# Chunk attention into a bilinear layer: one 256-token unit transposed by DMA, three small steps moved

## The chip, the cores and the metric

The kernel runs on one core of a Trainium2 chip. The metric is the device time of one execution in microseconds (us). Five engines work side by side, each from its own instruction queue and in that queue's order: TensorE (PE, with a separate row PEld for weight loads), VectorE (DVE), ScalarE (ACT), GpSimd (POOL) and SyncE (SP), which in this kernel only issues DMA transfers. Engines wait for each other by semaphores.

## The reference, cut to what matters

```
q, k, v: 8 x 8 x 576 x 64 (batch, head, position, feature), cut into chunks of 64 positions
scores = q_c @ k_c^T / 8;  attn = softmax(scores);  out = attn @ v_c      # per chunk and head
x = out as 4608 tokens x 512 (heads side by side)
a = x @ w_a;  b = x @ w_b            # w_a, w_b: 512 x 1536
result = (a * b) @ w_out             # w_out: 1536 x 512, result 4608 x 512 in float32
```

Inputs and result are float32. The kernel computes attention in bfloat16 and the layer in float16.

## The kernel before, in words

**Units and blocks.** The 4608 tokens are 18 units of 256 tokens for attention (U = 0 to 17) and 9 blocks of 512 tokens for the layer (K = 0 to 8); block K uses units 2K and 2K+1. `x_tiles[K]` (named xT in the profile) holds the attention result of a block, transposed.

**One unit's way.** `load(U)` (line 181) issues the DMA loads of q, k and v on SP into a staging pool `st`. `cast(U)` (L203) makes bfloat16 copies `q_raw`, `k_raw`, `v_raw` on POOL. Then q and k have to be transposed into `qkt`. Units below `PE_UNITS` are transposed on PE by `transpose_pe` (L217: 8 matmuls against an identity for q and 8 for k, one PSUM bank each; L225: two copies out of each bank, those of q on DVE and those of k on ACT). The other units are transposed by `transpose_dma` (L230), two DMA transposes on SP. For a PE unit `load` takes two neighbouring positions into one partition, 512 contiguous bytes (L188); for a DMA unit it takes one position per partition, 256 contiguous bytes (L176). After that: `scores` (L248 matmuls, L256 exponential on ACT), `sums` (L263 matmuls with ones, L273 logarithm on ACT), `inverse` (L282, exponential of the negated logarithm on ACT), `values` (L296 matmuls, L305 multiplication by the inverse on DVE, which writes xT). `bring(U)` (line 324) is, in this order: cast q and k of U, load q of U+1, DMA transposes of U, cast v of U, load k and v of U+1.

**The layer.** Block 0 runs in 12 whole steps `ab_step` (L355 matmuls, L363 copy on ACT, L364 product on DVE). Block 1 runs in 24 half steps `h` of 256 tokens each, the first 12 on unit 2's half of the block. Blocks 2 to 8 use a scheme of seven products (`Group`, L405 on PE; L416 and L423 copies on ACT; L443, L444 and L455 on DVE), for the output too (`OutGroup`, L541). That scheme needs sums of weights and of activations: `combine_w` (L129, DVE), `combine_wo` (L158, POOL), `combine_ab` (L485, POOL), `combine_x` (L385, DVE). Output of blocks 0 and 1 is plain (`out_part`, L609).

**What sets the order.** The order is written out by hand: each engine gets its instructions in program order, nothing reorders them. SP's queue holds all loads, all DMA transposes and nearly all stores (L489). POOL's queue holds all casts and all L158 and L485 combinations. `bank()` hands out PSUM banks in turn from the list `spread`; a bank's next user waits until its last reader is done. Raw copies and `qkt` have three buffers each, `st` has eight.

**Around the change.** The part of block 1 that follows block 0 reads:

```
spread[:] = [psum_t, psum_b]
h(1)
transpose_pe(3)
h(3)
scores(3)
...
transpose_pe(5)
h(1)
normalize(4)          # sums(4), inverse(4)
h(1)
scores(5)
```

In block 2, step i = 1 calls `bring(8)`, step i = 3 `bring(9)`; two or one `combine_wo` follow in each step. In block 3, step i = 1, POOL gets three `combine_ab`, then `bring(10)`, then the last three `combine_wo`, which overwrite the upper right quarter of the output weights in place. Product n = 3 of block 2's output (`OutGroup(2)`, two steps later) reads that quarter on PE.

Of the kernel before, what the change touches and what calls it, by code (L numbers as in the profile page):

```python
# [8 lines left out]


PE_UNITS = 6
AB_SCALE = 256.0
OUT_SCALE = 1.0 / AB_SCALE

# [2 lines left out]
def kernel(  # L17
# [46 lines left out]
    psum_a = ctx.enter_context(tc.tile_pool(name="psuma", bufs=1, space=PSUM))  # L64
    psum_b = ctx.enter_context(tc.tile_pool(name="psumb", bufs=2, space=PSUM))
    psum_c = ctx.enter_context(tc.tile_pool(name="psumc", bufs=1, space=PSUM))
    psum_o = ctx.enter_context(tc.tile_pool(name="psumo", bufs=1, space=PSUM))
    psum_q = ctx.enter_context(tc.tile_pool(name="psumq", bufs=1, space=PSUM))
# [11 lines left out]
    spread = [psum_t, psum_b, psum_a, psum_c, psum_t, psum_b, psum_o, psum_q]  # L80
# [5 lines left out]
    def bank(pool=None):  # L86
        if pool is None:
            pool = spread[0]
            spread.append(spread.pop(0))
        return pool.tile([128, 512], FP32, name=bank_names[id(pool)])  # L90
# [71 lines left out]
    def pieces(U):  # L162

        r, end = UNIT * U, UNIT * U + UNIT
        while r < end:
            b, s = divmod(r, S)
            n = min(S - s, end - r)
            yield r - UNIT * U, b, s, n
            r += n

    def load_natural(st, src, U):
        for r, b, s, m in pieces(U):
            while m:
                g, p = divmod(r, 128)
                n = min(128 - p, m)
                nc.sync.dma_start(  # L176
                    out=st[p:p + n, g], in_=src[b, :, s:s + n, :].rearrange("h p d -> p h d")
                )
                r, s, m = r + n, s + n, m - n

    def load(U, names="qkv"):

        for n in names if U < NU else "":
            src = {"q": q, "k": k, "v": v}[n]
            if U < PE_UNITS and n != "v":
                st = st_pool.tile([128, H, 2, D], FP32, name="st")
                for r, b, s, m in pieces(U):
                    nc.sync.dma_start(  # L188
                        out=st[r // 2:(r + m) // 2].rearrange("p h i d -> p h (i d)"),
                        in_=src[b, :, s:s + m, :].rearrange("h (p i) d -> p h (i d)", i=2),  # L190
                    )
                staged[n, U] = st.rearrange("p h i d -> p i h d")
            else:
                staged[n, U] = st_pool.tile([128, 2, H, D], FP32, name="st")
                load_natural(staged[n, U], src, U)

    def cast(U, names="qkv"):
        for n in names if U < NU else "":
            raw[n, U] = raw_pool.tile(
                [128, 2, H, D], BF16, name=f"{n}_raw"  # L200
            )
            eng = nc.vector if U == 0 and n != "v" else nc.gpsimd
            eng.tensor_copy(out=raw[n, U], in_=staged.pop((n, U)))  # L203
# [4 lines left out]
    def transpose_pe(U, names="qk"):  # L208
        if U not in qkt:
            qkt[U] = qkt_pool.tile([128, 2, 2, NKT, 128], BF16, name="qkt")  # L210
        for n in names:
            w = "qk".index(n)
            src = raw.pop((n, U))
            tp = bank().bitcast(BF16).rearrange("c (i m p) -> c i m p", i=2, m=NKT)
            for i in range(2):
                for m in range(NKT):
                    nc.tensor.transpose(  # L217
                        tp[:, i, m, :],
                        src[:, i, 2 * m:2 * m + 2, :].rearrange("p j d -> p (j d)"),
                        identity,  # L220
                    )
            dst = qkt[U][:, w].rearrange("c g m (p i) -> c i m g p", i=2)
            for i in range(2):
                cp = nc.vector.tensor_copy if w == 0 or U == 1 else nc.scalar.copy
                cp(out=dst[:, i], in_=tp[:, i].rearrange("c m (g p) -> c m g p", g=2))  # L225

    def transpose_dma(U):
        qkt[U] = qkt_pool.tile([128, 2, 2, NKT, 128], BF16, name="qkt")
        for w, n in ((0, "q"), (1, "k")):
            nc.sync.dma_start_transpose(  # L230
                out=qkt[U][:, w].rearrange("p g m c -> p (g m) c"),
                in_=raw.pop((n, U)).rearrange("p g h d -> p (g h d)"),
            )
# [24 lines left out]
    def sums(U, halves=None):  # L258
        E = E_of[U]
        sm = [bank() for _ in range(2)]  # L260
        for cl in range(2):
            for j in range(2):
                nc.tensor.matmul(  # L263
                    sm[cl][j * 64:j * 64 + 64, :],
                    ones[cl * 64:cl * 64 + 64, :],
                    E[cl * 64:cl * 64 + 64, j].rearrange("p m g s -> p (m g s)"),
                    start=True,
                    stop=True,
                )
        ln_of[U] = sm_pool.tile([128, 2, NKT, 128], FP32, name="ln")  # L270
        rs_of[U] = ln_of[U]
        for cl in range(2):
            nc.scalar.activation(  # L273
                out=ln_of[U][:, cl].rearrange("p m n -> p (m n)"), in_=sm[cl], func=AF.Ln
            )
            if halves:
                inverse(U, cl)

    def inverse(U, cl=None):

        for c in [slice(0, 2)] if cl is None else [cl]:
            nc.scalar.activation(  # L282
                out=rs_of[U][:, c], in_=ln_of[U][:, c], func=AF.Exp, scale=-1.0
            )

    def values(U):
        E, rs, vr = E_of.pop(U), rs_of.pop(U), raw.pop(("v", U))
        K, u = divmod(U, 2)
        if u == 0:
            x_tiles[K] = x_pool.tile([128, NKT, BLK], FP16, name="xT")  # L290
        av = [bank().rearrange("p (m g s) -> p m g s", m=NKT, g=2) for _ in range(2)]
        for m in range(NKT):
            for g in range(2):
                for cl in range(2):
                    for j in range(2):
                        nc.tensor.matmul(  # L296
                            av[cl][j * 64:j * 64 + 64, m, g, :],
                            vr[cl * 64:cl * 64 + 64, g, 2 * m + j, :],
                            E[cl * 64:cl * 64 + 64, j, m, g, :],
                            start=True,  # L300
                            stop=True,
                        )
        for cl in range(2):
            x = x_tiles[K][:, :, 256 * u:256 * u + 256]
            nc.vector.tensor_tensor(  # L305
                out=x.rearrange("p m (g c s) -> p m g c s", g=2, c=2)[:, :, :, cl, :],
                in0=av[cl],
                in1=rs[:, cl].rearrange("p m (g s) -> p m g s", g=2),
                op=MULT,
            )  # L310

    def slot(s=None, f=None):

        if s is not None and s >= NU:
            s = None
        if f is not None:
            sums(f)
            inverse(f)
        if s is not None:
            scores(s)  # L320
        if f is not None:
            values(f)

    def bring(U):

        if U >= NU:
            return
        cast(U, "qk")
        load(U + 1, "q")
        if U < NU:  # L330
            transpose_dma(U)
        cast(U, "v")
        load(U + 1, "kv")
# [285 lines left out]
    with tc.manual_schedule(  # L619
# [56 lines left out]
        def combo():  # L676
            if combos:
                combine_w(*combos.pop(0))

        for ft in range(NFT):  # L680
            ab_step(0, ft)
            if 3 <= ft < 10:
                combo()
            if ft == 6:
                transpose_pe(2)
            if ft == 8:
                slot(2)
            if ft == 10:
                slot(None, 2)

        cast(4)
        cast(5)
        load(6)

        outs = []

# [4 lines left out]
        def half(ft, u):  # L701
            ab_step(1, ft, 256 * u, 256 * u + 256)
            if ft > 9 if u == 0 else ft != 5 and ft != 9 and ft != 11:
                combo()
            if u == 1 and ft % 2 and ft > 2:
                combine_w(ft // 2 - 1, 3)
# [3 lines left out]
        def h(n=1):  # L710
            for _ in range(n):
                half(*halves.pop(0))
# [5 lines left out]
        def out_0(tg):  # L718
            for p in range(3):
                out_part(0, tg, p, psum_b)  # L720

        spread[:] = [psum_t, psum_b]
        h(1)
        transpose_pe(3)
        h(3)
        scores(3)
        h(3)
# [7 lines left out]
        h(2)  # L735
        scores(4)
        out_0(1)
        transpose_pe(5)
        h(1)
        normalize(4)  # L740
        h(1)
# [2 lines left out]
        values(4)  # L744
        bring(7)
        h(1)
        spread[:] = [psum_a, psum_q]
        normalize(5)
        out_0(2)
        spread[:] = [psum_t]  # L750
# [138 lines left out]
```

The softmax here doesn't subtract the row's maximum and nothing guards it: scores larger than these inputs give would overflow.

## Time and profile before

| | us |
|---|---|
| median of 6 runs | 310.41 (310.15 to 311.32) |
| the profiled execution's own time | 311.45 |
| its span, first to last instruction | 309.7 |
| PE busy in the span | 293.7 (95%) |
| DVE, ACT, POOL busy | 205.8, 194.0, 178.0 |
| TensorE clock granted | 1.0 throughout |

The profile is of one execution. Its time is the span and 1.75 us around it, and it is 1.04 us over the median. PE has the most work, so a change pays where PE stands idle or loses instructions. The kernel's first 110 us also keep the DMA queue nearly always busy: all weights and the first nine units arrive then. A line of the timeline gives the start, the duration, the engine, the source line, the operation, what it writes and reads, and in brackets the idle time before it with whatever ended it.

### The profile page before, as it was taken

To read this page: it belongs to the slowest core of one execution; us is meant where nothing else is said; L and a number is where in the kernel's file an instruction comes from. 1 tells how busy PE (TensorE), PEld (TensorE's weight loads), DVE (VectorE), ACT (ScalarE), POOL (GpSimd) and SP (SyncE) were. 2 spreads that over 40 slices of the span, in tenths; PEclk is the share of its full clock that TensorE was granted. 3 is DMA by queue.
4 is the path that set the end of the run, shared out by engine and by line. 5 is a ranking of instruction groups with operands and counts; after the bars stand their busy time and mean duration, and the time that the engine had idled before them with its cause. 6 is when DMAs were issued, how large, how long until landed. Compare 5 with 4: busy or idle time off the path is not lost.

```text
span 309.7 us, 8487 instructions
## 1 busy us (share of the span) xinstructions
PE 293.7 (95%) x3478; PEld 228.9 (74%) x3478; DVE 205.8 (66%) x342; ACT 194.0 (63%) x350; POOL 178.0 (57%) x168
## 2 busy tenths in 40 slices
PE   2879989999999999999999999999999999999995
PEld 1534557866566758888888888888888888888884
DVE  3345863967866687567757776777668766965872
ACT  1643557448575657666876686768676867566531
POOL 0656756544527688936782677277737711780560
PEclk9999999999999999999999999999999999999999
DMA  7999999899979993699539953994493000300025
GB/s 226 325 383 254 292 342 336 224 225 209 266 172 234 245 253 103 72 226 235 154 60 240 234 151 80 244 230 133 99 176 118 20 2 2 138 1 3 0 76 197
DMA packets 138887, 54.03 MB, mean 174 GB/s; under 512 B 114016, under 2 KB 132960, under 8 KB 138848
## 3 DMA queue, kind: packets, MB, share of 16 engines
q1 hardware_dynamic: 138704, 53.36, 72.0%
q8 instruction: 27, 0.44, 0.6%
q10 hardware_dynamic: 144, 0.13, 0.1%
q14 instruction: 12, 0.10, 0.1%
HBM read 37.75 MB, written 9.44 MB: 152 GB/s over the span
## 4 chain that ended last, share of the span: by engine, by line
PE 81%; DVE 5%; ACT 4%; POOL 4%; issue 2%; DMA 2%; SPq 0%; DVEq 0%; POOLq 0%; ACTq 0%
PE pb L405 17%; PE pc L405 11%; PE pa L405 10%; PE po L541 9%; PE pq L541 8%; PE pb L609 3%; PE pb L355 3%; PE pc L355 3%; PE po L355 3%; DMA st<-in_q_dram 2%; PE pq L355 2%; POOL so L485 2%; PE pa L355 2%; DVE s L385 1%; PE pt L296 1%
## 5 line engine op out<-in xcount | busy, mean ns | idle before, releaser
L405 PEld LDWEIGHTS <-t 128*128 128x128 f16 x504 | 48.3, 98 | 10.4 <-issue 4.4
L443 DVE TENSOR_TENSOR c_sb<-pc,v_sb 128x512 f32<-128x512 f32 x42 | 28.9, 687 | 35.5 <-ACT v_sb L416 34.0
L485 POOL TENSOR_TENSOR so<-ab_sb 128x512 f16<-128x512 f16 x20 | 23.1, 1153 | 50.1 <-DVE ab_sb L455 50.1
L405 PE MATMUL pb<-s,wa 128*128 128x256 f16 x336 | 50.7, 273 | 0.1
L405 PE MATMUL pa<-xT,wb 128*128 128x256 f16 x336 | 50.4, 273 | 0.0
L416 ACT COPY u_sb<-pb 128x512 f32<-128x512 f32 x42 | 24.7, 587 | 24.8 <-PE pb L405 23.5
L541 PEld LDWEIGHTS <-ab_sb 128*128 128x128 f16 x336 | 32.9, 98 | 4.2 <-issue 0.4
L405 PEld LDWEIGHTS <-wb 128*128 128x128 f16 x336 | 32.9, 98 | 4.0
L405 PEld LDWEIGHTS <-wa 128*128 128x128 f16 x336 | 31.0, 98 | 6.2 <-issue 0.2
L203 POOL CAST k_raw<-st 128x1024 bf16<-128x1024 f32 x17 | 17.8, 1048 | 28.6 <-DMA st<-in_k_dram 27.4
L455 DVE SCALAR_TENSOR_TENSOR ab_sb<-pc,c_sb 128x512 f16<-128x512 f32 x42 | 28.9, 689 | 6.8 <-PE pc L405 5.5
L455 DVE SCALAR_TENSOR_TENSOR ab_sb<-pb,b_sb 128x512 f16<-128x512 f32 x42 | 28.9, 688 | 3.0 <-PE pb L405 2.6
L423 ACT COPY pb<-pa 128x512 f32<-128x512 f32 x42 | 24.6, 586 | 8.9 <-PE pa L405 8.8
L416 ACT COPY v_sb<-pb 128x512 f32<-128x512 f32 x42 | 24.9, 592 | 8.1 <-PE pb L405 8.1
L416 ACT COPY b_sb<-pa 128x512 f32<-128x512 f32 x42 | 25.0, 595 | 7.7 <-PE pa L405 7.7
L444 DVE TENSOR_TENSOR pc<-pc,u_sb 128x512 f32<-128x512 f32 x42 | 29.0, 690 | 0.0
L305 DVE TENSOR_TENSOR xT<-pt,ln 128x512 f16<-128x512 f32 x30 | 19.4, 686 | 12.2 <-PE pt L296 12.2
L203 POOL CAST v_raw<-st 128x1024 bf16<-128x1024 f32 x18 | 18.9, 1049 | 14.3 <-DMA st<-in_v_dram 12.5
L541 PEld LDWEIGHTS <-so 128*128 128x128 f16 x252 | 24.6, 98 | 3.4 <-issue 0.5
L203 POOL CAST q_raw<-st 128x1024 bf16<-128x1024 f32 x17 | 18.0, 1058 | 14.6 <-DMA st<-in_q_dram 13.7
L405 PE MATMUL pc<-s,t 128*128 128x256 f16 x168 | 25.2, 273 | 0.9 <-DVE ab_sb L455 0.9
L405 PE MATMUL pb<-s,t 128*128 128x256 f16 x168 | 25.3, 273 | 0.4 <-ACT pb L423 0.4
(132 smaller groups left out, 580.4 us busy)
## 6 DMA issues: line engine op xcount, KB each, us to landing
out_dram<-o_sb SPq DMA_DIRECT2D x34, 256.0 KB, 3.3
st<-in_v_dram SPq DMA_DIRECT2D x32, 256.0 KB, 4.0
st<-in_q_dram SPq DMA_DIRECT2D x23, 256.0 KB, 4.5
st<-in_k_dram SPq DMA_DIRECT2D x23, 256.0 KB, 3.5
st<-in_moe_w_b_dram SPq DMA_DIRECT2D x6, 512.0 KB, 6.7
st<-in_moe_w_a_dram SPq DMA_DIRECT2D x6, 512.0 KB, 7.8
st<-in_moe_w_out_dram SPq DMA_DIRECT2D x6, 512.0 KB, 6.8
st<-in_q_dram SPq DMA_DIRECT2D x4, 512.0 KB, 6.0
```

Of the source, the lines that this page charges most:

```text
L203: eng.tensor_copy(out=raw[n, U], in_=staged.pop((n, U)))
L305: nc.vector.tensor_tensor(out=x.rearrange("p m (g c s) -> p m g c s", g=2, c=2)[:, :, :, cl, :], in0=av[cl], in1=rs[:, cl].rearrange("p m ...
L355: nc.tensor.matmul(ps[n], w_ab[n, i][:, kt, o:o + 128], xT[:, kt, c0:c1], start=(kt == 0), stop=(kt == NKT - 1),)
L405: nc.tensor.matmul(t[:, h * 256:h * 256 + 256], w[:, kt, h * 128:h * 128 + 128], x[:, kt], start=start and h == 0 and kt == 0, stop=h == 1 ...
L416: nc.scalar.copy(out=t, in_=src)
L423: nc.scalar.copy(out=self.B, in_=self.A)
L443: nc.vector.tensor_tensor(out=self.c, in0=self.C, in1=self.v, op=ADD)
L444: nc.vector.tensor_tensor(out=self.C, in0=self.C, in1=self.u, op=ADD)
L455: nc.vector.scalar_tensor_tensor(out=self.dst[:, :, c0:c0 + 256], in0=t.rearrange("p (h n) -> p h n", h=2), scalar=AB_SCALE, in1=o.rearran ...
L485: (eng or nc.gpsimd).tensor_tensor(out=o, in0=x0, in1=x1, op=op)
L541: nc.tensor.matmul(t[:, c0:c0 + 256], a[:, kt, th * 128:th * 128 + 128], w[:, kt], start=n in (0, 4) and first and kt == 0, stop=last and ...
L609: nc.tensor.matmul(out_ps[K, tg], ab_tiles[K][:, ft, tg * 128:tg * 128 + 128], wo_sb[:, ft], start=(ft == 0), stop=(ft == NFT - 1),)
```

## The change

Unit 5 goes from PE to DMA: `PE_UNITS` is 5, so its q and k are loaded 256 bytes at a time (four transfers in place of two), `transpose_pe(5)` is gone, and `bring(5)` takes the place of `cast(5)` and `load(6)`. SP's queue then holds: load q of unit 6, two DMA transposes of unit 5, load k and v of unit 6. POOL's queue keeps its order. In block 0, `sums(2)` and `inverse(2)` stand after step 9 and `values(2)` stays after step 10; on ACT the two logarithms and the inverse then stand ahead of step 10's copy. The eight PE transposes of q of unit 3, with their two DVE copies, stand ahead of block 1's first half step, those of k stay behind it. `sums(5)` takes its two banks from `psum_q` and `psum_o` in place of `psum_a` and `psum_q`.

```diff
-PE_UNITS = 6
+PE_UNITS = 5
...
             if ft == 8:
                 slot(2)
+            if ft == 9:
+                sums(2)
+                inverse(2)
             if ft == 10:
-                slot(None, 2)
+                values(2)
 
         cast(4)
-        cast(5)
-        load(6)
+        bring(5)
...
         spread[:] = [psum_t, psum_b]
+        transpose_pe(3, "q")
         h(1)
-        transpose_pe(3)
+        transpose_pe(3, "k")
...
         out_0(1)
-        transpose_pe(5)
         h(1)
...
-        spread[:] = [psum_a, psum_q]
+        spread[:] = [psum_q, psum_o]
         normalize(5)
```

## The prediction

> **What bounds the kernel now.** I read the page first, for who is busy:
>
> ```profile
> PE 293.7 (95%) x3478; PEld 228.9 (74%) x3478; DVE 205.8 (66%) x342; ACT 194.0 (63%) x350; POOL 178.0 (57%) x168
> ...
> DMA  7999999899979993699539953994493000300025
> ```
>
> PE is the bound over the whole, and the DMA queue is full for the first 15 of 40 slices (116 us). So I read PE's timeline there, for what the change can take:
>
> ```profile
> 43.50 0.60 PE L355 MATMUL pa<-xT,wb 128*128 128x256 f16 x4 [1.47 <-DVE xT L305]
> 43.94 0.60 PE L355 MATMUL pc<-xT,wa 128*128 128x256 f16 x4
> 44.37 0.61 PE L217 MATMUL pt<-identity,q_raw 128*128 128x128 bf16 x8
> ...
> 69.52 0.61 PE L217 MATMUL pt<-identity,q_raw 128*128 128x128 bf16 x8
> 69.97 0.61 PE L217 MATMUL pb<-identity,k_raw 128*128 128x128 bf16 x8
> 70.42 0.60 PE L355 MATMUL pq<-xT,wb 128*128 128x256 f16 x4
> ...
> 76.09 0.40 PE L263 MATMUL pa<-E,ones 64*64 64x512 bf16 x2 [0.47 <-ACT v_sb L363]
> ```
>
> Three things are to be had: a 1.47 us hole at the start of block 1, 0.90 us of transposes (69.52 to 70.42), a 0.47 us hole. Then SP's timeline, for the queue that the transposes move into:
>
> ```profile
> 69.40 1.50 SPq L176 DMA_DIRECT2D st<-in_q_dram  x2
> 71.01 2.04 SPq L230 DMA_TRANSPOSE qkt<-q_raw  x1
> 73.15 1.24 SPq L230 DMA_TRANSPOSE qkt<-k_raw  x1
> 74.44 2.04 SPq L176 DMA_DIRECT2D st<-in_k_dram  x2
> ...
> 81.36 5.12 SPq L230 DMA_TRANSPOSE qkt<-q_raw  x1
> 86.59 1.25 SPq L230 DMA_TRANSPOSE qkt<-k_raw  x1
> ```
>
> SP issues back to back from 10 to 112 us: what goes in ahead delays all behind it. Last, who needs that stream on time (POOL's timeline, and PE's for the last line). Unit 6's transposes land at 77.5, PE reads them at 83.51; unit 7's at 89.8, read at 96.18: six us of slack. POOL, behind the casts, has none:
>
> ```profile
> 104.71 1.04 POOL L203 CAST v_raw<-st 128x1024 bf16<-128x1024 f32 x1 [0.88 <-PE pb L405]
> 113.69 1.15 POOL L485 TENSOR_TENSOR so<-ab_sb 128x512 f16<-128x512 f16 x1 [0.96 <-DVE ab_sb L455]
> 118.48 1.16 POOL L485 TENSOR_TENSOR so<-ab_sb 128x512 f16<-128x512 f16 x1 [1.30 <-DVE ab_sb L455]
> 128.23 3.38 POOL L158 TENSOR_TENSOR wo<-wo 128x512 f16<-128x512 f16 x3
> 131.66 1.03 PE L541 MATMUL pq<-wo,so 128*128 128x256 f16 x8 [0.29 <-POOL wo L158]
> ```
>
> The cast at 104.71 is that of v of unit 9, loaded at 99.91 to 101.7 (the PE reader named had long ended; the landing, some 3 us later, fits). From its end at 105.75 POOL works without a pause but for 0.96 and 1.30 us, and PE waits for its last piece at 131.6. The chain of waits runs through POOL there as well. From 132 to 200 PE is busy 68.00 of 68.00 us, so a shift at 131.6 reaches the end whole.
>
> [...] the pairs of units 8 and 9 hold SP 4.5 and 5.0 us, and two pairs leave holes (below). [...] The trace: q and k of unit 5 landed 1.5 us apart (61.1, 62.6; 512 KB each), the halves of v 0.95 us per 256 KB.
>
> **The change part by part.**
>
> *Sums of unit 2.* The hole's chain is sums 39.48, logarithms 39.95, inverse 41.07 to 42.13, xT on DVE 42.16 to 43.45. Moved up one step (1.73 us), sums stand at 37.75, logarithms at 38.2, inverse ends near 40.35. But step 10's copy (0.58) is now behind it on ACT, step 10's product (0.69) behind that on DVE, and the xT multiplications behind that: 40.35 + 0.55 + 0.65 + 1.3 gives 42.9, not 41.7. Gain 0.6 of the 1.47, bounds 0.2 and 1.0.
>
> *q of unit 3 ahead of block 1.* Its 8 transposes take 0.45 us on PE and fall into what is left of the hole; the cast ended at 40.88, PE is free at 41.9. Their DVE copies (1.35) now precede the first half step's product, whose bank PE wants at 45.5; it is free near 45.1. Gain 0.45, at worst 0.
>
> *Unit 5 off PE.* 16 transposes less, 0.90 us; ACT and DVE lose copies of 1.33 and 1.35, which were off the path.
>
> *Banks of sums 5.* The 0.47 us wait was for the bank written just before. psum_q has rested; psum_o's product on DVE follows an ACT copy behind unit 5's exponential. I take 0.25, bounds 0 and 0.47.
>
> Sum on PE: 0.6 + 0.45 + 0.90 + 0.25 = 2.2 us.
>
> *Unit 5's transposes in time?* q and k of unit 5 cost 0.8 us more of stream (2 x (1.9 - 1.5)), so unit 6's q is issued by 65.0 rather than 64.2, and the transposes follow. Issued like unit 6's (2.0 + 1.25), with landings like its pair's (6.4 after the first issue) or unit 8's (6.2), they land near 71.3. PE, 1.95 us early by then, asks at 72.70 - 1.95 = 70.75. Scores wait 0.4 (0 to 1.5), behind which all of PE stands. PE is then 1.8 us ahead.
>
> *The stream behind.* The pair holds SP 3.4 us (unit 6) to 6.5 (unit 7), 2.6 with an empty queue: I take 3.6. With 0.8 that is 4.4. Unit 6's k took 2.99 us to issue against a full queue where three such issues take 1.85 at their shortest;[...] so about 1.2 comes back. k, v of unit 6 and all of unit 7 run 3.2 us late. That alone eats half the slack of unit 6's scores, and none is lost. But two holes lie in this stream, shown by the windows (core 0: PE, PEld, DVE, ACT, POOL busy, clock, DMA share, GB/s):
>
> ```profile
> 75.00:76.00 1.00, 0.62 (x6) 0.39 (x4) 0.65 (x2) 1.00 (x4) 0.17 (x1) 1.00 0.29 6
> 85.00:87.00 2.00, 1.93 (x20) 1.39 (x18) 0.99 (x2) 2.00 (x5) 0.38 (x1) 1.00 0.13 12
> ```
>
> Both follow DMA transposes into which a 16 KB packet of the instruction queue (q8) fell; a third, at 107.4, too. Unit 8's pair met none and left no such hole. From pair end to pair end, unit 6 to 7 takes 13.45 us, 7 to 8 10.77, 8 to 9 10.44. Shifted transposes may miss those packets: of the 3.2 us, up to 2.4 would be made good. I put the lateness of v of unit 9 at 0.8 without holes, 2.1 with one, 3.2 or more with both.
>
> *POOL.* What it is late at 105.75 it makes up by its two pauses, 2.26 us, since DVE and PE are ahead. The end moves by the later of the two: PE's -1.8, or lateness - 2.26.
>
> Without holes 0.8 - 2.26 = -1.5: POOL, not PE, sets it, and PE waits 0.3 us there besides the old wait. On the profiled execution 311.45 - 1.5 = 309.95; on the median, 1.04 lower, 308.9. I shade to 309.1 for the possible wait before scores 5.
>
> **The rivals.** *Half the gain eaten:* one hole stays, lateness 2.1, the end moves by -0.15: 310.3. For it: eight of the twelve pairs leave a hole of over 1 us with such a packet in it or just before it, so four pairs in a row (units 5 to 8) without one would be luck. *Slower:* both holes stay or another comes with unit 5's pair, lateness over 2.9; v of unit 9 is then cast at 107.9 or later, and the last combination (L158) ends past 132.2. At 3.2 the end moves by +0.9 (311.3), at 4.5 by +2.2 (312.6). It decides from 2.26 us of lateness on, whatever PE gained. *The hole doesn't close:* the copy on ACT or the product on DVE holds xT to 43.4; 0.6 is lost from PE's 1.8, and POOL still allows -1.2: 309.2, so this hardly shows.
>
> **How the numbers follow.** 0.2% is 0.62 us, about what these runs tell from no change. No holes or nearly so (end by -0.62 to -2.2): 0.47. One hole (within 0.62): 0.25. Late by more than 2.9: 0.28. The low end is PE's whole sum, 310.41 - 2.2 = 308.2; I take 308.1. The high end, lateness 3.9, is 312.0; beyond both I leave 2 in 10. The likeliest case alone has 308.2 to 309.8.
>
> **What would show it.** Right: block 1's first half step at 42.9 behind q's transposes, scores 5 with a wait under 1.5 us, v of unit 9 cast by 106, PE's wait for wo (L158) near 0.6 and not much more. Wrong: that wait at 2 us or over, with the cast at 107 or later; or a wait of PE before scores 5 or 6 of over 2 us, which would put transposes and not POOL on the path; or new DMA holes at unit 5's pair.

## The result, and the profile after

The changed kernel takes 312.58 us (median of 16 runs, 311.33 to 314.74); the kernel before, on the same chips, 310.76 us (35 runs). The ratio is 1.0058, with a 95% interval of 1.0043 to 1.0073: slower, by 1.8 us. The profiled execution took 312.28 us itself, with a span of 310.5 us and the clock at 1.0. It lies 0.3 us under the median of its kernel; that of before, 311.45 us, lay 1.04 us over the median of 6 runs and lies 0.69 us over that of the 35. So the two profiled executions differ by 0.83 us only.

The page of the changed kernel, busy time and the row of the DMA queue by slices:

```profile
PE 293.8 (95%) x3462; PEld 227.9 (73%) x3462; DVE 202.8 (65%) x340; ACT 192.8 (62%) x348; POOL 177.6 (57%) x168
...
DMA  7999899999999995699549954995493000300024
```

PE executes 16 matmuls less and is busy for as long. Its timeline, with the idle time before an instruction in brackets:

```profile
42.68 0.61 PE L217 MATMUL pt<-identity,q_raw 128*128 128x128 bf16 x8
...
43.48 0.60 PE L355 MATMUL pa<-xT,wb 128*128 128x256 f16 x4 [0.19 <-DVE xT L305]
...
112.72 0.60 PE L405 MATMUL pc<-s,t 128*128 128x256 f16 x4 [0.79 <-DVE ab_sb L455]
...
118.66 0.60 PE L405 MATMUL pc<-s,t 128*128 128x256 f16 x4 [0.54 <-DVE ab_sb L455]
...
132.14 1.03 PE L541 MATMUL pq<-wo,so 128*128 128x256 f16 x8 [0.73 <-POOL wo L158]
```

The hole of 1.47 us at the start of block 1 is down to 0.19, the wait before sums 5 is gone, and PE's row shows none before scores 5. New are the wait at 118.66, and 0.73 instead of 0.29 us for wo. The wait near 113 was there before:

```profile
113.66 0.60 PE L405 MATMUL pc<-s,t 128*128 128x256 f16 x4 [0.74 <-DVE ab_sb L455]
```

SP's timeline of the changed kernel (start, how long the issue held the queue), the transposing pairs of units 5, 6 and 7:

```profile
66.64 1.34 SPq L230 DMA_TRANSPOSE qkt<-q_raw  x1
68.08 1.24 SPq L230 DMA_TRANSPOSE qkt<-k_raw  x1
...
76.19 1.66 SPq L230 DMA_TRANSPOSE qkt<-q_raw  x1
77.95 1.25 SPq L230 DMA_TRANSPOSE qkt<-k_raw  x1
...
85.71 3.15 SPq L230 DMA_TRANSPOSE qkt<-q_raw  x1
88.96 1.25 SPq L230 DMA_TRANSPOSE qkt<-k_raw  x1
```

Unit 6's pair ends at 79.20 us (74.39 before), unit 7's at 90.21 (87.84). From pair end to pair end it takes 11.0 us where it took 13.45, so the long stall of 5.12 us is gone; the stream is late all the same. POOL, behind it:

```profile
107.23 1.04 POOL L203 CAST v_raw<-st 128x1024 bf16<-128x1024 f32 x1 [0.83 <-PE pc L405]
...
115.28 1.15 POOL L485 TENSOR_TENSOR so<-ab_sb 128x512 f16<-128x512 f16 x1
...
118.98 1.15 POOL L485 TENSOR_TENSOR so<-ab_sb 128x512 f16<-128x512 f16 x1
...
128.71 3.38 POOL L158 TENSOR_TENSOR wo<-wo 128x512 f16<-128x512 f16 x3
```

The cast of v of unit 9 is 2.52 us later than before. The two pauses of 0.96 and 1.30 us that POOL had ahead of its sums of AB (the middle two lines) are used up, and its last sum of Wo still ends 0.48 us later.

**Where the time goes.** Start times in PE's timeline, counted from the start of block 0's last whole step (its Wb product) in each execution, so that a late start cancels. "No u5" is the changed kernel with unit 5 back on PE, "only u5" is the kernel before with unit 5 alone by DMA, "Wo early" the changed kernel with three sums of Wo moved on POOL; all three come below.

| | before | after | no u5 | only u5 | Wo early |
|---|---|---|---|---|---|
| block 1 | 3.37 | 2.53 | 2.54 | 3.37 | 2.54 |
| scores of unit 5 | 32.57 | 30.82 | 31.29 | 32.27 | 30.40 |
| scores of unit 8 | 71.80 | 70.00 | 70.71 | 71.28 | 69.58 |
| scores of unit 9 | 88.94 | 88.13 | 86.95 | 89.51 | 87.91 |
| scores of unit 10 | 105.31 | 104.96 | 102.98 | 106.30 | 103.82 |

PE is 1.80 us ahead up to unit 8, and has 0.35 us of that left two units later. From unit 10 to unit 17 (251.19 and 251.67 us) before and after take 105.75 and 105.76 us. So the lead is lost between 111 and 133 us. Two things lie outside the table. Block 0's last step, from which it counts, starts 4.76 us after the scores of unit 2 with the moved sums and 4.58 without, so 0.18 us of the lead is lost ahead of it. And the scores of unit 2 start at 36.19 us in the profiled execution of the changed kernel and at 35.55 in that of before: the two executions are 0.64 us apart where the two kernels are still the same.

### The profile page after: what moved, and what is told of

It reads as the page before. It is cut to its first block, busy times and chain, and to the rows that moved or that the text cites. A ratio compares the mean times of both kernels' runs of the same rounds, so it can differ in the third digit from the quotient of the medians.

```text
span 310.5 us, 8452 instructions
## 1 busy us (share of the span) xinstructions
PE 293.8 (95%) x3462; PEld 227.9 (73%) x3462; DVE 202.8 (65%) x340; ACT 192.8 (62%) x348; POOL 177.6 (57%) x168
## 4 chain that ended last, share of the span: by engine, by line
PE 66%; POOL 10%; DMA 10%; DVE 4%; issue 3%; SPq 3%; ACT 3%; POOLq 0%; ACTq 0%; DVEq 0%
PE pb L405 15%; PE pc L405 10%; PE po L541 9%; PE pa L405 9%; PE pq L541 8%; PE pb L609 3%; POOL so L485 3%; DMA st<-in_moe_w_b_dram 3%; DMA st<-in_v_dram 3%; DMA st<-in_k_dram 2%; POOL wot L158 2%; DMA st<-in_q_dram 2%; PE po L355 2%; SPq L176 2%; PE pt L263 1%
## 5 line engine op out<-in xcount | busy, mean ns | idle before, releaser
L443 DVE TENSOR_TENSOR c_sb<-pc,v_sb 128x512 f32<-128x512 f32 x42 | 28.9, 687 | 37.9 <-ACT v_sb L416 34.6
L455 DVE SCALAR_TENSOR_TENSOR ab_sb<-pc,c_sb 128x512 f16<-128x512 f32 x42 | 28.9, 689 | 6.7 <-PE pc L405 5.1
L455 DVE SCALAR_TENSOR_TENSOR ab_sb<-pb,b_sb 128x512 f16<-128x512 f32 x42 | 28.9, 688 | 3.6 <-PE pb L405 3.2
L444 DVE TENSOR_TENSOR pc<-pc,u_sb 128x512 f32<-128x512 f32 x42 | 29.0, 690 | 0.0
L405 PE MATMUL pc<-xT,t 128*128 128x256 f16 x168 | 25.2, 272 | 0.2
```

Of the source, the lines that this page charges most:

```text
L405: nc.tensor.matmul(t[:, h * 256:h * 256 + 256], w[:, kt, h * 128:h * 128 + 128], x[:, kt], start=start and h == 0 and kt == 0, stop=h == 1 ...
L443: nc.vector.tensor_tensor(out=self.c, in0=self.C, in1=self.v, op=ADD)
L444: nc.vector.tensor_tensor(out=self.C, in0=self.C, in1=self.u, op=ADD)
L455: nc.vector.scalar_tensor_tensor(out=self.dst[:, :, c0:c0 + 256], in0=t.rearrange("p (h n) -> p h n", h=2), scalar=AB_SCALE, in1=o.rearran ...
```

## The experiments

### Which part of the change, and which door

The first four ran on one chip, five rounds each; the kernel before was at 310.98 us there (59 runs).

**Unit 5 back on PE**, the other edits kept.

```diff
-PE_UNITS = 5
+PE_UNITS = 6
...
-        bring(5)
+        cast(5)
+        load(6)
...
         out_0(1)
+        transpose_pe(5)
```

> The kernel after, with unit 5 back on PE; the earlier sums of unit 2, the transposes of unit 3's q ahead of block 1 and the rested banks stay. Theory 'POOL chain' (DMA transposes of unit 5 delay the load stream, which delays v of unit 9 and with it the POOL work that PE waits for at 132): the stream is as before, so PE's own gain shows: 1.0 to 1.5 us under before, ratio 0.995 to 0.997. Theory 'moved steps' (the earlier sums or the moved transposes cost time on ACT or DVE): still 1 us or more over before. Theory 'late scores' (PE waits for unit 5's transposes themselves): under before too, so this run does not part it from the first.

Measured: 310.34 us (22 runs, 309.23 to 311.76), ratio 0.9980 [0.9967, 0.9993]. PE's and POOL's timelines of its profiled execution:

```profile
42.76 0.60 PE L355 MATMUL pa<-xT,wb 128*128 128x256 f16 x4 [0.19 <-DVE xT L305]
...
74.64 0.40 PE L263 MATMUL pq<-E,ones 64*64 64x512 bf16 x2 [0.19 <-ACT u_sb L363]
```

```profile
100.09 1.04 POOL L203 CAST v_raw<-st 128x1024 bf16<-128x1024 f32 x1 [1.21 <-PE pa L405]
...
126.01 3.37 POOL L158 TENSOR_TENSOR wo<-wo 128x512 f16<-128x512 f16 x3
```

PE keeps its gain of 1.1 us up to unit 8, POOL's cast comes 7.1 us earlier than in the changed kernel, and PE's row shows no wait from 84 to 140 us. The profiled execution, 309.23 us, is the fastest of the 22, so its stream need not be the usual one. By the times, the three small edits together are worth 0.2% (less than the 0.3 to 0.5% expected), and it is unit 5's transposes that lose it. It is the fastest kernel of this study; the three edits were not tried one by one.

**Unit 5 by DMA alone**, in the kernel before.

```diff
-PE_UNITS = 6
+PE_UNITS = 5
...
-        cast(5)
-        load(6)
+        bring(5)
...
-        transpose_pe(5)
```

> The kernel before, with unit 5 alone moved to DMA. 'POOL chain': as slow as the kernel after or nearly, 1.2 to 2.2 us over before, since PE's other gains were lost there anyway. 'Moved steps': within 0.6 us of before or faster. 'Late scores': slower by the wait before scores of unit 5, which the profile shows as an idle PE near 72; in the profile of the kernel after there is none.

Measured: 312.77 us (8 runs), ratio 1.0068 [1.0041, 1.0095]. PE's timeline:

```profile
113.09 0.60 PE L405 MATMUL pc<-s,t 128*128 128x256 f16 x4 [1.02 <-DVE ab_sb L455]
...
119.14 0.60 PE L405 MATMUL pc<-s,t 128*128 128x256 f16 x4 [0.66 <-DVE ab_sb L455]
...
132.34 1.03 PE L541 MATMUL pq<-wo,so 128*128 128x256 f16 x8 [0.72 <-POOL wo L158]
```

The same three waits as in the changed kernel, and the same time within the intervals. POOL's cast of v of unit 9 was at 106.48 us. PE's row shows no wait before scores 5, so the transposes land in time.

**The last three sums of Wo ahead of unit 10's casts**, in the changed kernel: on POOL the sums go ahead of three casts, which take 3.0 us, at the place where PE waits.

```diff
+                if K == 3 and i == 1:
+                    while wo_sums:
+                        combine_wo(*wo_sums.pop(0))
                 if i in (1, 3):
                     bring(2 * K + 4 if i == 1 else 2 * K + 5)
...
-                if K == 3 and i == 1:
-                    while wo_sums:
-                        combine_wo(*wo_sums.pop(0))
```

> The kernel after, with the last three combinations of output weights (POOL) put ahead of the three casts of unit 10 in block 3. 'POOL chain': those casts (2.96 us) leave the chain, PE's wait at 132 goes, and the time falls by 1.5 to 3 us under the kernel after, to 309.6 to 311.0. Theory 'PE is late by itself' (PE loses its time before block 3 and the wait for POOL is a by-product): within 0.7 us of the kernel after.

Measured: 311.42 us (20 runs, 309.75 to 314.88), ratio 1.0025 [1.0003, 1.0047]. By the ratios that is 1.0 us under the changed kernel (1.0058 [1.0043, 1.0073], on other chips); the intervals just overlap, and the gain lies between the two theories, 1.5 us or more and 0.7 or less. PE's timeline:

```profile
111.83 0.60 PE L405 MATMUL pc<-s,t 128*128 128x256 f16 x4 [1.00 <-DVE ab_sb L455]
...
117.76 0.60 PE L405 MATMUL pc<-s,t 128*128 128x256 f16 x4 [0.54 <-DVE ab_sb L455]
```

The wait for wo is gone (the sums end at 128.3 us), the other two stay. POOL's lateness seems to reach PE by two doors, then: the wait for wo, and the product on DVE that frees the bank pc.

**The same in the kernel before.**

> The kernel before with the same three combinations ahead of unit 10's casts. 'POOL chain': PE and POOL are balanced there before, with a wait of 0.29 us, so 0 to 0.7 us under before. 'PE is late by itself': the same as before.

Measured: 311.05 us (22 runs), ratio 0.9996 [0.9981, 1.0011]. Without unit 5 in the DMA stream the wait for wo is worth nothing that can be measured. Its profiled execution, 311.24 us, also shows that POOL can be late with unit 5 on PE: the cast of v of unit 9 came at 106.06 us, and PE waited 1.06 us near 114.

### How POOL holds up DVE

The product that PE waits for at 112 us stands on DVE behind two of the four sums of X (`combine_x`, L385). DVE's timeline of the changed kernel, and what POOL did in the same time:

```profile
109.77 1.00 DVE L385 TENSOR_TENSOR s<-xT 128x512 f16<-128x512 f16 x1
110.81 1.26 DVE L385 TENSOR_TENSOR s<-s,xT 128x512 f16<-128x512 f16 x1
112.00 0.68 DVE L455 SCALAR_TENSOR_TENSOR ab_sb<-pc,c_sb 128x512 f16<-128x512 f32 x1
...
116.63 1.37 DVE L385 TENSOR_TENSOR s<-xT,s 128x512 f16<-128x512 f16 x1
```

```profile
108.23 2.27 POOL L158 TENSOR_TENSOR wot<-wo,wot 128x512 f16<-128x512 f16 x2
110.46 1.33 POOL L485 TENSOR_TENSOR so<-ab_sb 128x512 f16<-128x512 f16 x1
```

With unit 5 on PE and the small edits kept, the same two sums and the same product:

```profile
109.76 0.41 DVE L385 TENSOR_TENSOR s<-xT 128x512 f16<-128x512 f16 x1
110.21 0.42 DVE L385 TENSOR_TENSOR s<-s,xT 128x512 f16<-128x512 f16 x1
110.55 0.69 DVE L455 SCALAR_TENSOR_TENSOR ab_sb<-pc,c_sb 128x512 f16<-128x512 f32 x1
```

There POOL was idle from 109.86 to 111.31 us. In the kernel before it was not, and there the first two sums were long already; only the other two were shorter than in the changed kernel, where they took 1.00 and 1.37 us:

```profile
110.76 0.96 DVE L385 TENSOR_TENSOR s<-xT 128x512 f16<-128x512 f16 x1
111.75 1.26 DVE L385 TENSOR_TENSOR s<-s,xT 128x512 f16<-128x512 f16 x1
...
116.64 0.82 DVE L385 TENSOR_TENSOR s<-xT 128x512 f16<-128x512 f16 x1
117.39 0.41 DVE L385 TENSOR_TENSOR s<-xT,s 128x512 f16<-128x512 f16 x1
```

So the wait near 113 us (0.74 before, 0.79 after) is old; the later two sums go with the new wait at 118.66. In the changed kernel POOL's pair ends at 110.50 and DVE's first sum at 110.77; POOL's next ends at 111.79 and DVE's second at 112.07: each of DVE's sums ends some 0.27 us after the POOL instruction beside it. None of the 128x512 operations on DVE with one operand in PSUM (L443, L444, L455) takes more than 0.69 us in the traces of before and after. In the changed kernel DVE's sums last until just behind the end of POOL's instructions, up to 1.37 us in place of 0.41.

To make POOL busy there without making it late, a base was needed in which POOL has time. **All units on PE**: no DMA transposes at all, and so a stream that runs early.

```diff
-PE_UNITS = 5
+PE_UNITS = 18
...
-        if U < NU:
-            transpose_dma(U)
...
+                ((2, 0), transpose_pe, U + 1),
                 ((2, 1), scores, U + 1),
...
+                ((5, 0), transpose_pe, U + 2),
```

(and unit 5 and unit 6 transposed on PE in block 1).

> The changed kernel with every unit transposed on PE and loaded in rows of 512 bytes: a stream with no transposing transfer in it, as a base for the two kernels that follow. 13 more units of 16 transposes cost PE some 13 x 0.90 = 11.7 us against the changed kernel: 320 to 326 us. Theory 'POOL late, DVE held up': with a stream that runs early POOL has its pauses back when DVE makes the sums of X for block 3, which take 0.41 us each there, and PE has no wait for ab_sb above 0.2 us and none for wo between 110 and 140 us. If the sums take 1.0 us or more although POOL is idle beside them, the theory falls.

Measured: 322.2 us (2 runs). The sums of X take 0.41, 0.42, 0.41 and 0.41 us, POOL is idle beside them, and PE has no wait from 86 to 145 us. As expected, no more than that: it is the base.

**Three idle sums on POOL** beside the sums of X; **three ahead of the last sums of Wo**; **17 of them behind unit 9's casts**, so that POOL runs late and without a pause; and the last one with the sums of X moved behind the product. The idle sums write a tile that nothing reads.

```diff
+    def fill(n):
+        for _ in range(n):
+            nc.gpsimd.tensor_tensor(
+                out=pad, in0=wo_sb[:, 0:2, 0:256], in1=wo_sb[:, 2:4, 0:256], op=ADD
+            )
...
+                if (K, i) == (2, 4):
+                    fill(17)              # third and fourth kernel
+                if (K, i) == (2, 5):
+                    fill(2)               # first
                 if K == 3 and i == 1:
+                    fill(3)               # second
...
                     finish(last)
+                    if (K, i) == (2, 5):
+                        fill(1)           # first
...
-                ((5, 0), lambda u: combine_x(u // 2, (0, 1)), U + 1),
+                ((5, 1), lambda u: combine_x(u // 2, (0, 1)), U + 1),      # fourth
```

(in the fourth, also part 3 of `combine_x` one half step later.)

> The kernel with all units on PE, with three idle sums (fp16, 128x512, into a tile that nothing reads) added on POOL where it has a pause while DVE makes the sums of X for block 3: two behind the sum of Wo at 111.58 us, one behind the sum of AB at 117.74 us. The pauses there are 2.66 and 1.31 us and the fillers take 1.15 each, so nothing on POOL comes later. Theory 'DVE held up by POOL': DVE's four sums go from 0.41 us to 1.0 us or more each, and PE gets waits for ab_sb of about 1.0 and 0.5 us: 1.0 to 1.6 us over the kernel without fillers (322.2). Theory 'only POOL's lateness counts': no change, within 0.3 us.

> The same base, with three idle sums on POOL just ahead of the last three sums of Wo: these end at 136.7 us instead of 133.34, and PE wants the last at 133.73. No sum of DVE that PE waits for lies beside them. Theory 'POOL chain': PE waits about 3.0 us for wo, and the time is 3.0 us over the base (325.2): POOL's lateness beyond its slack reaches the end one for one. If PE finds other work or the wait is made good later: under 2 us.

> The same base, with 17 idle sums on POOL behind the sum of Wo at 94.8 us: POOL starts its first sum of AB near 114.9 us instead of 108.12 and runs from there without a pause, as it does in the changed kernel behind the cast of v of unit 9. The last sum of Wo ends near 136.2. Theory 'POOL chain', the two doors in series: PE's waits for ab_sb (1.0 and 0.5 us) come first, the wait for wo takes the rest, and the sum of the three is 2.5 us: 324.7. Theory 'additive': the waits for ab_sb on top of it: 326 or more.

> The kernel before it in this list, with the four sums of X on DVE moved behind the multiplication that frees PE's bank. Theory 'in series': the waits for ab_sb shrink, the wait for wo grows by as much, the time stays within 0.3 us of the kernel without the move (324.7). Theory 'additive': 1.0 to 1.5 us less than that.

These four ran on another chip than the base, where the kernel before was at 312.43 us instead of 310.92, so their medians (323.63, 327.04, 327.57 and 329.41 us; 1.0374, 1.0476, 1.0508 and 1.0552 of before) can't be set against the base's directly (1.0368 of before, from 2 runs, with an interval of 1.0321 to 1.0414). By these ratios alone the first kernel could not be told from the base. Base, first and second kernel were run once more on one chip:

> The base with all units on PE once more, on one chip with the two that follow, because the first time it ran on another chip than they did, where the kernel before differs by 1.5 us. Its own spread was 0.1 us, while that of the kernel before is 1.5 us or more. Theory 'the spread is the stream's' (the transposing pairs make the stream's pace vary, and POOL's end with it): 322 to 324 us by chip, with less than 0.5 us between its lowest and highest. Otherwise its spread is as wide as that of before.

> Three idle sums on POOL beside the sums of X on DVE, on the same chip as the base. In the profiled execution two of DVE's four sums went from 0.42 to 1.26 and 1.38 us, and PE waited 0.96 us at the scores of unit 7, behind a copy that DVE made late. Theory 'DVE held up by POOL': 0.9 to 1.2 us over the base. Theory 'only POOL's lateness counts': within 0.3 us.

(The wait of which this speaks stood at the scores of unit 8, not 7.)

> Three idle sums on POOL ahead of the last three sums of Wo, on the same chip as the base. In the profiled execution PE waited 2.34 us for wo and lost 2.8 us in all, at full clock; four of five executions without the profiler were 2.2 to 2.8 us longer than that one, with a mean granted clock of 0.995. Theory 'lateness one for one': 2.8 us over the base. Theory 'the wait costs clock as well': 4.4 to 5.5 us over the base in the executions at 0.995 (0.5% of 325 us is 1.6 us), 2.8 in those at 1.0.

Measured, before at 311.20 us:

| | us (runs) | ratio to before | PE, from block 2's first product of sums (Group) to scores of unit 10, us |
|---|---|---|---|
| base | 322.08 (4) | 1.0350 [1.0330, 1.0371] | 63.67 |
| idle sums beside the sums of X | 323.88 (5) | 1.0415 [1.0395, 1.0436] | 64.72 |
| idle sums ahead of Wo | 325.81 (5) | 1.0465 [1.0444, 1.0486] | 66.51 |

*Beside the sums of X.* DVE's, POOL's and PE's timelines of this kernel in its second run (L383 are the sums of X here, L164 the idle sums):

```profile
113.75 1.26 DVE L383 TENSOR_TENSOR s<-s,xT 128x512 f16<-128x512 f16 x1
...
120.62 1.38 DVE L383 TENSOR_TENSOR s<-xT,s 128x512 f16<-128x512 f16 x1
```

```profile
113.36 2.66 POOL L164 TENSOR_TENSOR warm_in<-wo 128x512 f16<-128x512 f16 x2
...
120.35 1.37 POOL L164 TENSOR_TENSOR warm_in<-wo 128x512 f16<-128x512 f16 x1
```

```profile
116.40 0.45 PE L248 MATMUL pt<-qkt 64*64 64x64 bf16 x32 [0.97 <-DVE qkt L233]
```

Two of the four sums of X got three times as long, not all four, and PE waited once, for a copy of q of unit 8 that stands behind them on DVE. The stretch of PE from block 2 to scores 10 is 1.05 us longer, with POOL never late at wo. POOL's idle sums alone cost the time, so that a sum on POOL holds up a sum on DVE, and PE behind it, is shown; by what means is not. The medians differ by 1.8 us, more than the expected 0.9 to 1.2; the two profiled executions by 1.3, of which 0.44 is a later start of block 2. I put this door at 1.05 us here; what else parts the medians is open.

*Ahead of Wo.* PE's timeline, second run:

```profile
135.55 0.38 PE L539 MATMUL pq<-wo,so 128*128 128x256 f16 x2 [0.85 <-POOL wo L158]
...
136.67 0.38 PE L539 MATMUL pq<-wo,so 128*128 128x256 f16 x2 [0.73 <-POOL wo L158]
...
137.78 1.03 PE L539 MATMUL pq<-wo,so 128*128 128x256 f16 x8 [0.73 <-POOL wo L158]
```

PE's stretch is 2.84 us longer; POOL's last sum of Wo ends 51.7 us after block 2's start where it ended at 48.05 in the base, 3.6 us later. In the base PE reads that sum 0.8 us after it is ready (the sum ends at 133.57 us; the fifth of the twelve products that start at 133.95 reads it, near 134.4). Less this slack the lateness goes through one for one. PE waits for each of the three sums in turn.

*Late and without a pause.* With 17 idle sums (1.24 us each, not the 1.15 counted on) PE's stretch is 69.65 us, and with the sums of X moved away from the product 69.54. The waits in the first are 1.38 us for the copy on DVE, 0.34 for the product and 0.71, 0.74, 0.73 for wo; in the second all of it is for wo, and the first wait there is

```profile
137.74 0.38 PE L539 MATMUL pq<-wo,so 128*128 128x256 f16 x2 [3.03 <-POOL wo L158]
```

So the two doors stand in series: as long as POOL's queue is full up to its last sum of Wo, its end decides, and what DVE no longer loses PE loses at wo. In the changed kernel itself this was not measured: there is no time for it with the sums of X moved, nor with both moves. In the median the fourth kernel is even 1.8 us longer than the third, which no theory had. Of the 1.8 us between their profiled executions, 0.98 is a later start of block 2, ahead of anything in which the two differ, and 0.93 comes behind the scores of unit 10, with 0.59 at one wait for DVE at 288 us: there the moved sums of the later blocks cost time. The clock, next, falls by as much in both (to 0.50).

### The clock behind a wait

The windows of the third kernel (PE, PEld, DVE, ACT, POOL busy, granted clock, DMA share, GB/s):

```profile
136.00:138.00 2.00, 0.76 (x4) 0.38 (x4) 1.30 (x2) 0.59 (x2) 2.00 (x3) 1.00 0.68 153
138.00:140.00 2.00, 1.49 (x9) 1.13 (x9) 0.00 (x0) 0.00 (x0) 2.00 (x3) 0.70 0.04 8
140.00:142.00 2.00, 2.00 (x12) 0.91 (x11) 0.69 (x1) 1.02 (x2) 1.41 (x2) 0.50 0.00 0
142.00:144.00 2.00, 2.00 (x19) 1.74 (x18) 0.69 (x1) 1.80 (x5) 0.00 (x0) 0.94 0.00 0
```

Behind the waits the clock falls to 0.50. Shares of 0.30, 0.50 and 0.06 of 2 us each are missing: 1.7 us lost, or, as an estimate, 3.4 us at half clock. From 140 to 142 us 12 matmuls run, and 21 from 144 to 146 at full clock. The fall came although PE was busy for 0.76 us of the two from 136 to 138, and for 1.49 of the next two. In whole executions it shows as a mean clock of 0.995 (0.5% of 325 us is 1.6). With the idle sums ahead of Wo, on one chip, two executions at clock 1.0 took 325.16 us each and three at 0.995 took 325.81, 326.32 and 326.85: 0.7 to 1.7 us more, or 3.1 and 3.7 to 4.8 over the base (2.8 and 4.4 to 5.5 expected); the waits of these three were not profiled. One of the two at 1.0 was, with waits of 0.85, 0.73 and 0.73 us and no fall. All four executions of the fourth kernel were at 0.994 or less, and two of four of the third, where the clock does not sort the times: 327.44 and 327.66 us at 1.0, 327.48 and 329.10 at 0.995.

In the profiled execution of the changed kernel the clock stays at 1.0 behind its waits of 0.79, 0.54 and 0.73 us. But its longest execution, 314.74 us, and two of the kernel with early sums of Wo, 314.13 and 314.88, have a mean clock of 0.995, which none of the 59 of the kernel before has. That POOL was later still in these is argued, not shown.

The theory that the spread comes from the stream is not borne out: the base without a transposing transfer ran from 321.72 to 323.25 us, the kernel before beside it from 310.95 to 311.80.

## Why the prediction was wrong

Forecast: 309.1, faster; it is 312.58, beyond the high end of 312.0. By its time the case that came is the rival "slower", given 0.28; the lateness of the profiled execution, 2.52 us, lies under the 2.9 that this rival named.

**Bounds and chain: right.** The prediction had POOL, from the cast of v of unit 9 on, as the path, and PE's wait for wo as the place where it reaches the end. The kernels made from before and after and the idle sums say so. Its marks for "wrong" were the cast at 107 or later with a wait of 2 us or more; the cast came at 107.23, the wait at 0.73, since PE had lost part of its lead before: of the 1.80 us at the scores of unit 8, 0.81 is left at those of unit 9, and 0.54 went at the new wait for the bank pc.

**PE's sum: right in total, in part by luck.** 1.8 us ahead at block 2 was forecast, 1.80 is measured at scores 8. At scores 3 the sums of unit 2 and q's transposes have brought 1.28 (1.05 forecast; 1.10 when the 0.18 us ahead of the table is taken off), and unit 5's transposes bring 0.88 (0.90). The banks of sums 5 bring nothing for 0.25: the first sum no longer waits, but the second starts 0.46 us behind it (0.01 before). The wait before scores 5, put at 0.4, is 0.2 at most: at 71.76 us the load of their weights on PEld ends a wait of 0.21 us for the transposes of k. What is missing instead, 0.41 us, went between scores 3 and scores 4; the kernel with the early sums of Wo, the same up to there, didn't lose it and is 2.22 us ahead at scores 8.

**The stream: the term that was too small.** The prediction's term is the lateness of the cast of v of unit 9: 3.2 us put in by the pair and the packets, 2.4 made good by holes that vanish, 0.8 left. The 3.2 is 4.4 less 1.2 that was to come back behind the pair, which was an estimate; k of unit 6 took 1.95 us to issue there (SP, at 69.37 us), 1.04 less than the 2.99 before. Measured for the term are 2.52. The table follows the stream in the two profiled executions (end of the issue on SP, us):

| | before | after | late | late, less the 0.86 at the start |
|---|---|---|---|---|
| v of unit 4 (before unit 5's loads) | 54.94 | 55.80 | 0.86 | 0 |
| v of unit 6 | 69.31 | 73.42 | 4.11 | 3.25 |
| pair of unit 6 | 74.39 | 79.20 | 4.81 | 3.95 |
| pair of unit 7 | 87.84 | 90.21 | 2.37 | 1.51 |
| v of unit 9 | 101.73 | 103.96 | 2.23 | 1.37 |

*Pair and packets: 3.2, then 3.95.* At v of unit 6 the lateness is 3.25 us, as forecast; by the end of unit 6's pair, still ahead of both holes of before, it has grown to 3.95. Against the two other kernels with unit 5 on PE it is 3.3 us there (Wo early in the kernel before: 54.85 to 74.91) and 5.1 (53.64 to 71.95); unit 5 alone by DMA takes 23.26 us where the changed kernel takes 23.40. The packets are what they were put at: k of unit 5 is cast 1.87 us after q in the changed kernel and 1.50 before, both as soon as they land, 0.4 per tensor and 0.8 for both. What is over, in the pair and in what runs beside it, is the larger part. The packets alone and the pair alone have no time, so how the 3.95 divides stays open.

*"Made good" by holes that vanish: right.* From pair to pair of units 6 and 7 the lateness falls by 2.44 us; 2.4 was forecast. In the changed kernel the DMA engines are busy where the two holes of before lay (windows; columns as in the prediction, the last but one is the DMA share):

```profile
75.00:76.00 1.00, 0.94 (x7) 0.41 (x5) 1.00 (x4) 0.91 (x2) 0.05 (x1) 1.00 1.13 250
85.00:87.00 2.00, 2.00 (x17) 1.40 (x16) 0.25 (x1) 2.00 (x5) 1.12 (x2) 1.00 1.06 318
```

With unit 5 on PE and the small edits kept there are holes too, elsewhere and shorter:

```profile
82.00:83.00 1.00, 0.95 (x37) 0.70 (x36) 1.00 (x3) 0.82 (x2) 0.34 (x1) 1.00 0.06 6
93.00:93.75 0.75, 0.75 (x9) 0.67 (x8) 0.75 (x2) 0.16 (x1) 0.75 (x2) 1.00 0.08 9
```

The kernel before with early sums of Wo has them at 75.5 to 76.5 and 85.0 to 86.5 us (shares of 0.06 and 0.08). From v of unit 4 to v of unit 9 all three profiled executions with unit 5 on PE have such holes (0.75 us or more with a share under 0.1), and none of the three with it by DMA has. But fewer holes did not make the stream early: over this stretch the first three take 46.8, 48.0 and 43.1 us, the other three 48.2, 48.4 and 48.7.

*What no term held.* The stream of the changed kernel was 0.86 us late before the first of unit 5's loads; the kernel with unit 5 on PE, the same up to there, had it at 53.64, so the start differs by 2.2 us between two executions of the same code. And the cast comes 0.29 us later behind its loads' issue than before. The cast of v of unit 9 was at 104.71, 106.06 and 100.09 us in the three kernels with unit 5 on PE, and at 107.23, 106.48 and 106.33 in those with it by DMA: later, but with a spread that one profile of each doesn't give away.

*This is the step that failed:* the lateness of v of unit 9, put at 0.8 us and measured at 2.52. Of the 1.72 us between, 0.86 is the start of the stream, 0.57 what unit 5 itself cost over the forecast (1.37 left for 0.8), and 0.29 lies between issue and cast. The forecast for the profiled execution was 309.95, and it is 312.28: besides the 1.72 us, POOL made up 0.22 less than its pauses, and 0.35 comes after the scores of unit 17.

*A second step, from the profile to the median, adds 1.34:* minus 1.04 was taken, plus 0.30 is right. The 1.04 rests on 6 runs; against the 35 it is 0.69. To subtract it supposes that what made this execution slow leaves the changed kernel as well. The prediction had already let its two holes go, and if they were what made it slow, the same was counted twice; that they were is not shown. Why the medians lie 1.8 us apart and the profiled executions 0.83 stays open.

**POOL's pauses: right, but not free.** Lateness less 2.26 us of pauses gives 0.26 with the measured lateness; the last sum of Wo came 0.48 later. In the second pause DVE ran its fourth sum of X at 0.41 us before; with the pause gone, the third and fourth took 1.00 and 1.37 for 0.82 and 0.41, and PE got its second wait for pc. The prediction saw slack there and didn't ask who used it. With idle sums on POOL this was in series with the wait for wo and didn't add to it; that it is so in the changed kernel too is argued. With the wait for wo removed, this wait remained.

**The rivals.** "Half the gain eaten" and "the hole doesn't close" didn't come. "Slower" was priced at 311.3 for 3.2 us of lateness, 0.9 over the median of before; over the profiled execution, without the subtraction, it would have been 312.35.

## What to carry to other kernels

What was put into the busy DMA stream here was paid at its consumer, POOL: the cast of v of unit 9 came 2.52 us later, 1.37 us of it behind unit 5's transfers. What a transfer puts in and what it takes away are two terms: here the holes went as forecast (2.44 us made good), and the stream was late all the same. One profiled execution gives neither term its spread: two executions of the same code had their streams 2.2 us apart before the changed part came, so a lateness read from one pair of profiles, and the distance from a profile to a median of six runs, need a second execution before they are added up. A pause of POOL was worth more than its idle time here: a sum of X on DVE took 0.41 us in it and 1.37 without it. On a PE that was busy for 95% of the span, freeing 0.9 us by unit 5's DMA transposes made the kernel some 2 us slower (ratios to before of 1.0058 with them, 0.9980 without); try the small edits without the large one first.

## What the runs showed of the hardware

A DVE sum of two float16 operands in SBUF (128x512) took 0.41 to 0.42 us with POOL idle and up to 1.38 beside a POOL sum; a 128x512 DVE operation with one operand in PSUM (L443, L444, L455) stayed at 0.68 to 0.69 in before and after. The clock fell to 0.50, for some 3.4 us by estimate from the 1.7 us lost, behind three waits of 0.71 to 0.74 us with work between in one profiled execution, and stayed at 1.0 behind waits of 0.73 to 0.85 in another. And the kernel before differs by 1.5 us between two chips (310.92 us, 3 runs, and 312.43, 7 runs), so kernels that are to be compared to half a per cent have to share one.
